# An MLP fused by row blocks, weight gradients as filler beside spectral stages, and transposes by DMA

## The chip, the cores and the metric

The kernel runs on one core of one Trainium2 chip. The metric is the device time of one execution in microseconds, the median of the runs shown.

## What is computed

A block with two halves, forward and backward (all gradients but that of B_x). With x of 2048 rows by 512 and mod = silu(c) @ w_mod, six vectors of 512 (sa, ca, ga, sb, cb, gb):

```python
h = _layernorm(x) * (1 + ca) + sa
x = x + ga * irfft2(rfft2(h) * (w_r + 1j * w_i))       # spectral half
h = _layernorm(x) * (1 + cb) + sb
r = relu(h @ w1 + b1)                                   # MLP half, 512 -> 1792 -> 512
x = x + gb * ((r * r) @ w2 + b2)
_out, _vjp = jax.vjp(_f, A_x, A_w_r, A_w_i, B_w1, B_b1, B_w2, B_b2, c, w_mod)
```

The inputs and outputs are bf16; grad_out goes into the vjp.

## The kernel before

TensorE is called PE here, VectorE DVE, ScalarE ACT, GpSimd POOL, SyncE SP. Rows are held as 128 partitions by 16 row tiles t; the inner width 1792 is 14 chunks fc of 128, the outer width 512 four chunks dc. Tiles are placed and ordered by a framework: the program gives each instruction an engine and a priority (its place in the text, unless changed), and the order on each engine's queue is fixed when the program is built. Every DMA is issued from SP's queue.

The 2D FFTs are matmuls with sine tables. F1 (`spec_f1`) multiplies each row tile by TA; F2 and F3 (`spec_f23`) go over eight pairs of frequencies, with PSUM tiles psB and psC, and end in an elementwise complex product (`cmul`); G1 (`spec_g1`) writes CS; G2 and G3 (`spec_g23`) turn CS into row tiles, psT and psY. The tables LF, LG, Cf and Cd are made at the start (`build_lf`, `build_lg`, `build_cf`, `build_cd`), written to DRAM and loaded again for the backward half.

The stages run one after the other:

1. Layernorm of x, F1, the six vectors, the tables; F2, F3 and G1 forward.
2. G2, G3, the residual and the second layernorm, row by row (`y_cons`, L632). Each four rows are transposed on PE into h2T.
3. h = w1 * h2T for all 14 fc (L683), relu into rT (L686), square into hactT (L687), rT to DRAM (L690).
4. out = hactT * w2 (L725) row by row, with column sums by matmuls with ones (L740, L743). Transposes of w2 (L720) and of gB = grad_out * gb (L746) on PE.
5. For each fc: psg = w2T * gBT (L784), ghT = 2 * rT * psg (L787), rT transposed back on PE (L797), copied (L798), squared (L800), and the gradient of w2 (L803). The transpose of w1 (L812).
6. gh * w1^T row by row (L843) with the layernorm's backward and three column sums.
7. `emit_gmod_chunk` for the vectors sb, cb and ga: their part of the gradient of w_mod and of c. (gb is done after stage 4, sa and ca at the end.)
8. In two halves: ghT transposed on PE (L891), copied (L893, L896), and the gradient of w1 (L902), written out by L911.
9. Backward: tables reloaded, F1 to G1 with two complex products per pair (`ew_bwd`), then G2, G3 and the first layernorm's backward row by row (`gh1_cons`, L960), and the last two `emit_gmod_chunk`.

Of the kernel before, what the change touches and what calls it, by code (L numbers as in the profile page):

```python
# [43 lines left out]
def build_basic(tc, constp, g):  # L44
# [37 lines left out]
def build_ta(tc, K, cpool, g, pspool):  # L82
# [15 lines left out]
    TA = cpool.tile([P, P], BF16, name="TA")  # L98
# [3 lines left out]
    TAT = cpool.tile([P, P], BF16, name="TAT")  # L102
# [4 lines left out]
def build_cd(tc, K, g):  # L107
    nc = tc.nc
# [10 lines left out]
    v = g.tile([P, 4, D], I32, name="cd_v")  # L119
    for c in range(4):  # L120
        nc.vector.scalar_tensor_tensor(out=v[:, c, :], in0=fr, scalar=d2[:, c:c + 1], in1=off, op0=ALU.mult, op1=ALU.add)
    nc.vector.tensor_single_scalar(v, v, 1023, op=ALU.bitwise_and)
    sn = g.tile([P, 4, D], FP32, name="cd_sn")
    nc.scalar.activation(sn, v, AF.Sin, scale=TWO_PI / 1024, bias=K["npi"])
# [4 lines left out]
def build_cf(tc, K, cpool, g):  # L129
    nc = tc.nc  # L130
    dr = g.tile([P, D], I32, name="cf_dr")
    nc.gpsimd.iota(dr, pattern=[[2, D]], base=1, channel_multiplier=0)
    f4 = g.tile([P, 4], FP32, name="cf_f4")
    for i, b in enumerate((0, 128, 1, 129)):
        nc.vector.tensor_scalar(f4[:, i:i + 1], K["pidf"], float(b), None, op0=ALU.add)
    efc = g.tile([P, 4], FP32, name="cf_ef")
    nc.vector.memset(efc, EF_S)
    nc.vector.tensor_scalar(efc[:, 0:1], K["pidf"], 0.0, EF_S * (math.sqrt(0.5) - 1.0), op0=ALU.is_equal, op1=ALU.mult)
    nc.vector.tensor_scalar(efc[:, 0:1], efc[:, 0:1], EF_S, None, op0=ALU.add)
    nc.vector.tensor_scalar(efc[:, 3:4], K["pidf"], 127.0, EF_S * (math.sqrt(0.5) - 1.0), op0=ALU.is_equal, op1=ALU.mult)  # L140
    nc.vector.tensor_scalar(efc[:, 3:4], efc[:, 3:4], EF_S, None, op0=ALU.add)
    v = g.tile([P, 4, D], I32, name="cf_v")
    for i in range(4):
        nc.vector.tensor_scalar(v[:, i, :], dr, f4[:, i:i + 1], 768.0 if i < 2 else 512.0, op0=ALU.mult, op1=ALU.add)
    nc.vector.tensor_single_scalar(v, v, 1023, op=ALU.bitwise_and)
    sn = g.tile([P, 4, D], FP32, name="cf_sn")
    nc.scalar.activation(sn, v, AF.Sin, scale=TWO_PI / 1024, bias=K["npi"])
    Cf = cpool.tile([P, 4, D], BF16, name="Cf")
    for i in range(4):
        nc.vector.tensor_scalar(Cf[:, i, :], sn[:, i, :], efc[:, i:i + 1], None, op0=ALU.mult)  # L150
    K["Cf"] = Cf


def build_lf(tc, K, cpool, g):
    nc = tc.nc
    sm = g.tile([P, 16, 8], FP32, name="lf_sm")
# [38 lines left out]
    c, s = tr
    LF = cpool.tile([P, 6, 16, P], BF16, name="LF")
    L5 = LF.rearrange("p y g (a b) -> p y g a b", b=8)
    for y, (w, m) in enumerate(((c, 0), (s, 1), (s, 2), (c, 2), (c, 1), (s, 3))):
        nc.vector.tensor_tensor(L5[:, y], w, mk[:, m, :, None, :].broadcast_to([P, 16, 16, 8]), op=ALU.mult)
    for y, w, z in ((2, c, z0), (3, s, z0n), (5, c, z0n)):  # L200
        nc.vector.tensor_scalar(L5[:, y, 0, :, 4], w[:, 0, :, 4], z, None, op0=ALU.mult)
    K["LF"] = LF


def build_lg(tc, K, cpool, g):
    nc = tc.nc
    lam = K["lowf"]
    rl = g.tile([P, 1], FP32, name="lg_rl")
    nc.gpsimd.tensor_scalar(rl, lam, -1.0, 7.0, op0=ALU.mult, op1=ALU.add)
    e4 = g.tile([P, 1], FP32, name="lg_e4")  # L210
    nc.gpsimd.tensor_scalar(e4, lam, 4.0, None, op0=ALU.is_equal)
    e0 = g.tile([P, 1], FP32, name="lg_e0")
    nc.gpsimd.tensor_scalar(e0, lam, 0.0, None, op0=ALU.is_equal)
    ge4 = g.tile([P, 1], FP32, name="lg_ge4")
# [148 lines left out]
def spec_g23(tc, K, CS, consumer):  # L363
    nc = tc.nc
    with tc.tile_pool(name="tsb", bufs=3) as tpool, \
# [8 lines left out]
        for t in range(NT):  # L374
# [6 lines left out]
            if prev is not None:  # L381
                g3(*prev)
# [655 lines left out]
```

## Time and profile before

| | us |
|---|---|
| median of 3 runs | 773.96 (772.61 to 774.38) |
| the profiled execution, its own time | 772.14 |
| its span in the trace | 770.4 |
| PE busy | 576.6 (75%) |
| DVE busy | 445.3 (58%) |
| ACT busy | 251.4 (33%) |
| DMA queue, share of 16 engines | 36.8%, 92.2 MB |

Busy time is the time in which an engine has an instruction in work. Matmuls are pipelined, so a row's mean time of one is longer than the distance from one to the next. The granted clock (PEclk) is the share of 2.4 GHz that PE was given.

### The profile page before, as it was taken

The numbers are of one execution on the slowest core, as the hardware profiler recorded it, in microseconds if no ns is written. First come the engines' busy times: TensorE is split into PE (matmuls) and PEld (weight loads), VectorE is DVE, ScalarE is ACT, GpSimd is POOL, SyncE is SP. The second block draws the span as 40 slices with busy tenths as digits, with TensorE's granted clock in tenths as the row PEclk, the third lists the DMA queues.
The fourth block names the chain that finished last, engine by engine and source line by source line (L and its number), as shares of the span: only waits on it lengthen the run. The fifth ranks groups of instructions, "written<-read, shape, count | busy, mean of one in ns | idle before, by whom it ended". The sixth has DMA issues, their size and how long they took to land. (4 is left out here: it accounts for less than half of the span.)

```text
span 770.4 us, 9001 instructions
## 1 busy us (share of the span) xinstructions
PE 576.6 (75%) x3190; PEld 278.1 (36%) x3190; DVE 445.3 (58%) x1126; ACT 251.4 (33%) x404; POOL 48.6 (6%) x138
## 2 busy tenths in 40 slices
PE   1364997457999995999999879955989369397530
PEld 0221683123444332445444323313555146262100
DVE  7977456655744445544554469983131039649981
ACT  2454546335664111223323201113231045144210
POOL 6531002310000000000000000000000000000000
PEclk9995999858999998999999979975999779799855
DMA  7208964577334231412221252321008780321110
GB/s 300 82 27 321 227 158 139 177 210 254 137 136 137 83 101 56 165 69 76 95 71 42 43 163 83 102 75 43 25 25 328 234 250 1 129 91 42 41 54 27
DMA packets 70528, 92.78 MB, mean 120 GB/s; under 512 B 9938, under 2 KB 62804, under 8 KB 69460
## 3 DMA queue, kind: packets, MB, share of 16 engines
q1 hardware_dynamic: 70484, 92.22, 36.8%
q8 instruction: 25, 0.41, 0.2%
q14 instruction: 19, 0.16, 0.1%
HBM read 51.80 MB, written 40.39 MB: 120 GB/s over the span
## 5 line engine op out<-in xcount | busy, mean ns | idle before, releaser
L787 DVE SCALAR_TENSOR_TENSOR ghT<-rT_pf,twof,psg 128x512 bf16<-128x512 bf16 x56 | 40.7, 745 | 55.8 <-PE psg L784 55.6
L784 PE MATMUL psg<-gBT,w2T 128*128 128x512 bf16 x224 | 60.2, 387 | 1.8 <-ACT gwm L439 1.8
L683 PE MATMUL psH<-h2T,w 128*128 128x512 bf16 x224 | 55.1, 402 | 5.2 <-ACT rT L686 4.4
L843 PE MATMUL psh<-w1T,ghT 128*128 128x512 bf16 x224 | 56.3, 392 | 0.4 <-DVE ghT L787 0.4
L902 PE MATMUL psw<-ghn,h2b 128*128 128x448 bf16 x256 | 52.0, 355 | 3.6 <-DVE gw L909 3.6
L725 PE MATMUL psO<-w,hactT 128*128 128x512 bf16 x224 | 53.5, 379 | 0.8 <-ACT rT L686 0.8
L803 PE MATMUL psw<-gB,hnat 128*128 128x512 bf16 x224 | 50.8, 380 | 0.5 <-DVE hnat L800 0.5
L686 ACT ACTIVATE rT<-psH,b1col 128x512 bf16<-128x512 f32 x56 | 38.4, 687 | 22.1 <-PE psH L683 17.4
L687 DVE TENSOR_TENSOR hactT<-rT 128x512 bf16<-128x512 bf16 x56 | 23.7, 424 | 25.3 <-ACT rT L686 25.2
L683 PEld LDWEIGHTS <-w 128*128 128x128 bf16 x224 | 22.7, 101 | 37.0 <-issue 16.3
L843 PEld LDWEIGHTS <-ghT 128*128 128x128 bf16 x224 | 20.0, 100 | 39.8 <-issue 21.6
L798 ACT COPY rnat<-pstr 128x512 bf16<-128x512 bf16 x56 | 29.9, 587 | 11.7 <-PE pstr L797 9.7
L902 PEld LDWEIGHTS <-h2b 128*128 128x128 bf16 x256 | 24.7, 99 | 24.7 <-issue 4.4
L805 ACT CAST gw<-psw 128x512 bf16<-128x512 f32 x14 | 8.2, 585 | 73.8 <-PE psw L803 68.5
L803 PEld LDWEIGHTS <-hnat 128*128 128x128 bf16 x224 | 20.8, 98 | 29.4 <-DVE hnat L800 6.2
L846 ACT CAST gh<-psh 128x512 bf16<-128x512 f32 x16 | 9.4, 585 | 63.2 <-PE psh L843 63.2
L784 PEld LDWEIGHTS <-w2T 128*128 128x128 bf16 x224 | 21.1, 99 | 23.2 <-issue 6.9
L909 DVE CAST gw<-psw 128x448 bf16<-128x448 f32 x8 | 5.0, 624 | 42.3 <-PE psw L902 25.3
L725 PEld LDWEIGHTS <-hactT 128*128 128x128 bf16 x224 | 20.2, 98 | 24.6 <-issue 4.2
L308 POOL MEMSET AE<- 128x2 bf16 x6 | 0.3, 107 | 453.7 <-PE psw L902 441.5
L730 DVE TENSOR_TENSOR bo<-psO,b2b 128x512 bf16<-128x512 f32 x16 | 11.1, 691 | 27.6 <-PE psO L725 27.6
L891 PE MATMUL pstg<-ident,ghT 128*128 128x128 bf16 x224 | 21.0, 242 | 7.7 <-DVE ghn L893 4.0
(326 smaller groups left out, 1084.4 us busy)
## 6 DMA issues: line engine op xcount, KB each, us to landing
rT_dram<-rT SPq DMA_DIRECT2D x14, 512.0 KB, 2.6
rT_pf<-rT_dram SPq DMA_DIRECT2D x14, 512.0 KB, 3.2
w<-in_B_w_dram SPq DMA_DIRECT2D x2, 1792.0 KB, 8.9
wm<-in_w_mod_dram SPq DMA_DIRECT2D x4, 768.0 KB, 10.0
LF_dram<-LF SPq DMA_DIRECT2D x1, 3072.0 KB, 10.3
LG_dram<-LG SPq DMA_DIRECT2D x1, 3072.0 KB
wmc_pf<-in_w_mod_dram SPq DMA_DIRECT2D x6, 512.0 KB, 10.8
out_dram<-gwm SPq DMA_DIRECT2D x24, 128.0 KB, 1.7
```

The source lines that it names most:

```text
L683: nc.tensor.matmul(psH, lhsT=w1[:, dc, fc * P:(fc + 1) * P], rhs=h2T[:, dc, sc * 4 * P:(sc + 1) * 4 * P], start=(dc == 0), stop=(dc == 3))
L686: nc.scalar.activation(rT[:, sc * 4 * P:(sc + 1) * 4 * P], psH, AF.Relu, bias=b1col[:, fc:fc + 1])
L687: nc.vector.tensor_tensor(hactT[fc][:, sc * 4 * P:(sc + 1) * 4 * P], rT[:, sc * 4 * P:(sc + 1) * 4 * P], rT[:, sc * 4 * P:(sc + 1) * 4 * P ...
L725: nc.tensor.matmul(psO, lhsT=hactT[fc][:, t * P:(t + 1) * P], rhs=w2[:, fc, :], start=(fc == 0), stop=(fc == NFC - 1))
L730: nc.vector.tensor_tensor(bo, psO, b2b, op=ALU.add)
L784: nc.tensor.matmul(psg, lhsT=w2T[:, dc, fc * P:(fc + 1) * P], rhs=gBT[:, dc, sc * 4 * P:(sc + 1) * 4 * P], start=(dc == 0), stop=(dc == 3))
L787: nc.vector.scalar_tensor_tensor(out=ghT[fc][:, sc * 4 * P:(sc + 1) * 4 * P], in0=rT[:, sc * 4 * P:(sc + 1) * 4 * P], scalar=K["twof"], in ...
L798: nc.scalar.copy(out=rnat[:, 4 * tg:4 * tg + 4, :], in_=pst.rearrange("p (j f) -> p j f", j=4))
L803: nc.tensor.matmul(psw2, lhsT=hnat[:, t, :], rhs=gB[:, t, :], start=(t == 0), stop=(t == NT - 1))
L843: nc.tensor.matmul(psh, lhsT=ghT[fc][:, t * P:(t + 1) * P], rhs=w1T[:, fc, :], start=(fc == 0), stop=(fc == NFC - 1))
L891: nc.tensor.transpose(pst[:, jj * P:(jj + 1) * P], ghT[fc][:, t * P:(t + 1) * P], K["ident"])
L902: nc.tensor.matmul(psw, lhsT=h2[:, t, dc * P:(dc + 1) * P], rhs=ghn[:, t, cc * 448:(cc + 1) * 448], start=(t == 0), stop=(t == NT - 1))
```

## The change

- g * w2^T is taken apart from the relu's derivative: `gaT = (2 gb w2)^T g` needs no forward result and is computed beside the forward spectral stages, with a priority of LATE behind all else. Its operands gT and w2T come by DMA with `transpose=True`.
- The MLP runs in four blocks of four row tiles: `stage_g` (G2, G3, second layernorm, h2T by PE as before), `stage_h` (h, relu, square, `gaT *= r`), `stage_o` (out, gh * w1^T, layernorm's backward, F1 of the backward half for the last blocks). w1T comes by DMA transpose and is scaled and centred in place, so that the layernorm's mean term needs no pass of its own. h and gh go to DRAM.
- The gradients of w1 and w2 are computed beside the backward spectral stages, again LATE, from h and gh loaded back by DMA transposes (ghn, hn). The column sums of sb and cb come out of w1's gradient instead of matmuls with ones.
- `GMod.emit` makes the gradient of w_mod by scaling one broadcast row on ACT in place of four outer products on PE.
- The tables are smaller (LF 4 rows and LFx, LG by windows and LGx) and made in pieces; the complex products take one tile per pair; column sums are issued some rows later (`Delayed`).

```diff
+class Priority:
...
+    def __enter__(self):
+        self.tc.cur_priority = self.tc.cur_priority + self.shift
...
+class Delayed:
...
+    def add(self, fn):
+        self.q.append(fn)
+        if len(self.q) > self.lag:
+            self.q.pop(0)()
...
+    def emit(self, jc, row_ap, pool, ppool, wmc):
+        psb = ppool.tile([P, D], FP32, name="mm")
+        nc.tensor.matmul(psb, lhsT=K["ones_row"], rhs=row_ap, start=True, stop=True)
...
+        nc.scalar.copy(out=gmbc, in_=psb)
...
+        for dc in range(4):
+            nc.scalar.activation(gwm[:, dc, :], psb, AF.Copy, scale=self.scf[:, dc:dc + 1])
+            nc.vector.scalar_tensor_tensor(out=junk, in0=wmc[:, dc, :], scalar=K["onef"], in1=gmbc, op0=ALU.mult, op1=ALU.mult,
+                                           accum_out=self.gsc[:, jc, dc:dc + 1])
+        nc.sync.dma_start(self.out9_view[:, :, jc * D:(jc + 1) * D], gwm)
...
+    for b in range(NB):
+        gT.append(w2gp.tile([P, 4, SB], BF16, name="gT", bufs=2))
+        for j in range(TB):
+            nc.sync.dma_start(gT[b][:, :, j * P:(j + 1) * P], g_view[:, TB * b + j, :], transpose=True)
+        if b == 0:
+            nc.sync.dma_start(w2T, B_w2, transpose=True)
...
+    with Priority(tc, LATE):
+        for dc in range(4):
+            nc.vector.tensor_scalar(w2T[:, dc, :], w2T[:, dc, :], gb2x[:, dc:dc + 1], None, op0=ALU.mult)
+        for b in range(NB):
+            for fc in range(NFC):
+                ps = mmps.tile([P, SB], FP32, name="mm")
+                for dc in range(4):
+                    nc.tensor.matmul(ps, lhsT=w2T[:, dc, fc * P:(fc + 1) * P], rhs=gT[b][:, dc, :], start=(dc == 0), stop=(dc == 3))
+                with tc.high_priority():
+                    if fc % 2 == 0:
+                        nc.vector.tensor_copy(out=gaT[fc][:, b * SB:(b + 1) * SB], in_=ps)
+                    else:
+                        nc.scalar.copy(out=gaT[fc][:, b * SB:(b + 1) * SB], in_=ps)
...
+    nc.sync.dma_start(w1T, B_w1, transpose=True)
...
+        def stage_h(b):
...
+            for fc in range(NFC):
+                ps = mmps.tile([P, SB], FP32, name="mm")
+                for dc in range(4):
+                    nc.tensor.matmul(ps, lhsT=w1[:, dc, fc * P:(fc + 1) * P], rhs=h2T[b][:, dc, :], start=(dc == 0), stop=(dc == 3))
...
+                nc.scalar.activation(r, ps, AF.Relu, bias=b1col[:, fc:fc + 1])
...
+                nc.vector.tensor_tensor(h, r, r, op=ALU.mult)
+                nc.sync.dma_start(h_dram[fc, :, sl], h)
+                nc.vector.scalar_tensor_tensor(out=gaT[fc][:, sl], in0=r, scalar=K["onef"], in1=gaT[fc][:, sl],
+                                               op0=ALU.mult, op1=ALU.mult, accum_out=gb1acc[:, fc, b:b + 1])
+                nc.sync.dma_start(gh_dram[fc * P:(fc + 1) * P, sl], gaT[fc][:, sl])
...
+        stage_g(0)
+        stage_g(1)
+        stage_h(0)
+        stage_o(0)
+        stage_g(2)
+        stage_h(1)
+        stage_o(1)
+        stage_g(3)
...
+    def grad_w2():
+        for fc in range(NFC):
+            hn = gwp.tile([P, NT, P], BF16, name="hn", bufs=2)
+            nc.sync.dma_start(hn, h_dram[fc, :, :], transpose=True)
+            ps = mmps.tile([P, SB], FP32, name="mm")
+            for t in range(NT):
+                nc.tensor.matmul(ps, lhsT=hn[:, t, :], rhs=g_sb[:, t, :], start=(t == 0), stop=(t == NT - 1))
+            gw = gwp.tile([P, D], BF16, name="gw", bufs=3)
+            with tc.high_priority():
+                nc.vector.tensor_tensor(gw, ps, modb[:, GB_B, :], op=ALU.mult)
+            nc.sync.dma_start(out6_view[:, fc, :], gw)
+    def grad_w1():
...
+        W4 = 256
+        for fb in range(F // W4):
+            ghn = gwp.tile([P, NT, W4], BF16, name="ghn", bufs=2)
+            nc.sync.dma_start(ghn, gh_dram[fb * W4:(fb + 1) * W4, :], transpose=True)
...
+            for dc in range(4):
...
+                    nc.tensor.matmul(ps[:, 0:W4], lhsT=n2_sb[:, t, dc * P:(dc + 1) * P], rhs=ghn[:, t, :],
+                                     start=(t == 0), stop=(t == NT - 1))
...
+    with Priority(tc, LATE):
+        for j, row in ((5, ggb_row), (2, gga_row)):
+            wmc = gm.prefetch(j, gwp)
+            gm.emit(j, row, gwp, mmps, wmc)
+        grad_w1()
...
+        spec_f23(tc, K, UT, CdB, None, lambda gi: fr.tile([P, 2, 2, FP], BF16, name="G"), ew_b)
...
+    spec_g1(tc, K, Z, CS)
...
+    with Priority(tc, LATE):
+        grad_mod_mid()
+        grad_w2()
```

Not shown of the diff: the tables, `stage_g` and `stage_o` (per row: o0 = o * gb + x1, gp = g * o, then cb, a scalar_tensor_tensor with the sum of cb * n2, u = rb * n2 + g, gx1 = u + cb, qy = gx1 * y), and the last rows' arithmetic, in which two scalar_tensor_tensors become tensor_tensors. In `stage_g` psT, psY and the transposes' pst2 have one PSUM buffer each, in F2 psB has one in place of two. w2, w1 and w1T are in the space of w2T, gT and the forward Z.

## Rows read from the trace of the kernel before

**Rows 1.** Busy time, granted clock and DMA by stage (start:end in us).
```profile
0.00:56.00 56.00, 20.32 (x120) 9.97 (x121) 47.08 (x117) 23.37 (x29) 30.19 (x85) 0.99 0.36 132
56.00:117.00 61.00, 48.15 (x321) 32.67 (x320) 35.91 (x81) 27.47 (x35) 4.82 (x19) 0.84 0.83 231
117.00:166.00 49.00, 26.03 (x144) 11.54 (x143) 32.84 (x89) 22.25 (x39) 13.44 (x32) 0.81 0.54 167
166.00:226.00 60.00, 54.77 (x232) 22.98 (x230) 32.81 (x88) 37.78 (x56) 0.00 (x0) 0.90 0.53 193
226.00:298.00 72.00, 68.69 (x371) 28.68 (x370) 34.15 (x82) 18.22 (x34) 0.00 (x0) 1.00 0.31 101
298.00:308.00 10.00, 3.26 (x14) 1.02 (x14) 5.70 (x15) 1.52 (x3) 0.00 (x0) 0.65 0.16 53
308.00:431.00 123.00, 121.59 (x732) 59.24 (x732) 61.23 (x142) 37.71 (x70) 0.00 (x0) 0.99 0.24 82
431.00:505.00 74.00, 65.24 (x260) 21.29 (x258) 57.89 (x165) 9.95 (x17) 0.00 (x0) 0.93 0.37 105
505.00:530.00 25.00, 9.61 (x26) 2.27 (x26) 17.61 (x49) 5.46 (x10) 0.00 (x0) 0.58 0.22 74
530.00:605.00 75.00, 67.12 (x470) 40.37 (x470) 16.02 (x35) 20.25 (x36) 0.00 (x0) 0.93 0.31 122
605.00:622.00 17.00, 0.90 (x7) 0.39 (x6) 0.62 (x1) 0.00 (x0) 0.17 (x3) 0.59 0.98 268
622.00:657.00 35.00, 34.01 (x254) 23.58 (x252) 27.28 (x54) 20.80 (x31) 0.00 (x0) 0.95 0.28 84
657.00:686.00 29.00, 16.55 (x132) 13.77 (x131) 13.91 (x27) 4.95 (x10) 0.00 (x0) 0.76 0.37 146
686.00:740.00 54.00, 34.86 (x112) 9.34 (x112) 50.45 (x154) 18.12 (x33) 0.00 (x0) 0.85 0.10 34
740.00:770.40 30.40, 5.49 (x10) 0.99 (x9) 11.74 (x37) 3.51 (x6) 0.00 (x0) 0.50 0.13 43
sum 770.40, PE 576.59 PEld 278.09 DVE 445.27 ACT 251.36 POOL 48.63; mean PE 38.44 PEld 18.54 DVE 29.68 ACT 16.76 POOL 3.24
```
**Rows 2.** Pace of PE: timeline of F3, then chain of waits in the w1 gradient.
```profile
74.38 3.62 PE L317 MATMUL psC<-AE,LF 128*128 128x257 bf16 x16 [11.52 <-ACT AE L333]
...
80.19 1.95 PE L317 MATMUL psC<-AE,LF 128*128 128x257 bf16 x16
...
541.63 0.49 PE pstg L891 x8
542.12 0.57 PE psw L902 x3
...
546.12 20.63 PE psw L902 x109
```
**Rows 3.** Pace of DVE: timeline in the last rows, then a copy from the groups.
```profile
689.89 0.74 DVE L968 SCALAR_TENSOR_TENSOR gn<-psY,onef,modb 128x512 bf16<-128x512 f32 x1
690.56 0.08 DVE L968 DVE_READ_ACCUMULATOR gn<-psY,onef,modb 128x1 f32 x1
690.65 0.42 DVE L965 TENSOR_TENSOR q<-gh,n1b 128x512 bf16<-128x512 bf16 x1
690.99 0.74 DVE L971 SCALAR_TENSOR_TENSOR qn<-gn,onef,n1b 128x512 bf16<-128x512 bf16 x1
...
L358 DVE CAST CS<-psG 128x512 bf16<-128x512 f32 x8 | 5.5, 690 | 6.5 <-PE psG L351 6.5
```
**Rows 4.** DMA issues: times, KB each, median us from issue to landing.
```profile
out_dram<-gwm SPq DMA_DIRECT2D x24, 128.0 KB, 1.7
...
Wb<-in_A_w_i_dram SPq DMA_DIRECT2D x1, 1028.0 KB, 11.9
...
b1colb<-in_B_b_dram SPq DMA_DIRECT2D x1, 3.5 KB, 3.3
```
**Rows 5.** The chain that ended last: a store of w1's gradient.
```profile
584.23 8.45 DMA out_dram<-gw
```

More of the change, by code (lines that the diff above doesn't have):

```diff
@@ L24 @@
 NT = 16
+NB = 4
+TB = NT // NB
+SB = TB * 128
 P = 128
@@ L142, in build_cf @@
[L142 to L147, printed above, removed]
+    efc = g.tile([P, 2], FP32, name="cf_ef")
+    for i, edge in enumerate((0.0, 127.0)):
+        nc.vector.tensor_scalar(efc[:, i:i + 1], K["pidf"], edge, math.sqrt(0.5) - 1.0, op0=ALU.is_equal, op1=ALU.mult)
@@ L195, in build_lf @@
[L195 to L202, printed above, removed]
+    LF = cpool.tile([P, 4, 16, P], BF16, name="LF")
@@ L284, in spec_f1 @@
-def spec_f1(tc, K, row, UT):
-    nc = tc.nc
-    with tc.tile_pool(name="psA", bufs=3, space=PSUM) as psA_pool:
-        for t in range(NT):
-            hrow = row(t)
-            ps = psA_pool.tile([P, 4, P], FP32, name="psA")
-            for c in range(4):
-                nc.tensor.matmul(ps[:, c, :], lhsT=hrow[:, c * P:(c + 1) * P], rhs=K["TA"], start=True, stop=True)
-            dst = UT[:, :, :, t, :]
-            src = ps.rearrange("p c (a b) -> p c a b", b=8)
-            if t % 2 == 1:
-                nc.scalar.copy(out=dst, in_=src)
-            else:
-                nc.vector.tensor_copy(out=dst, in_=src)
+    mk = g.tile([P, 2, 6, 8], BF16, name="lg_mk")
@@ L300, in spec_f23, with spec_f1_row @@
+def spec_f1_row(tc, K, hrow, t, UT, pool, name):
+    nc = tc.nc
+    ps = pool.tile([P, 4, P], FP32, name=name)
+    for c in range(4):
+        nc.tensor.matmul(ps[:, c, :], lhsT=hrow[:, c * P:(c + 1) * P], rhs=K["TA"], start=True, stop=True)
+    dst = UT[:, :, :, t, :]
+    src = ps.rearrange("p c (a b) -> p c a b", b=8)
+    if t % 4 == 0:
+        nc.vector.tensor_copy(out=dst, in_=src)
+    else:
+        nc.scalar.copy(out=dst, in_=src)
 def spec_f23(tc, K, UT, Cd, dc, dest, elementwise):
@@ new lines, with grad_mod_mid @@
+    gsba = gwp.tile([P, 4, F // 256], FP32, name="gsba")
+    gcba = gwp.tile([P, 4, F // 256], FP32, name="gcba")
+    def grad_mod_mid():
+        for i, j in enumerate((3, 4)):
+            wmc = gm.prefetch(j, gwp)
+            psr = psX.tile([P, D], FP32, name="mm")
+            for dc in range(4):
+                nc.tensor.matmul(psr[0:1, dc * P:(dc + 1) * P], lhsT=colsb[:, i, dc:dc + 1], rhs=K["ident"], start=True, stop=True)
+            row = gwp.tile([1, D], BF16, name="gmrow")
+            nc.scalar.copy(out=row, in_=psr[0:1, :])
+            gm.emit(j, row, gwp, psX, wmc)
```

1292 lines of the change are left out of this document (590 added, 702 removed).

## The prediction

> **What bounds the kernel now.** I read the profile in this order: time by stage, the pace of TensorE (PE), the pace of VectorE (DVE), the DMA rows, the chain that ended last. In the table by stage [rows 1] the reader is to see that no engine bounds the whole: PE is busy 576.6 us of 770.4 and DVE 445.3, but they take turns. PE is full in the MLP stages (121.6 of 123 us in 308 to 431) and mostly idle in the setup, where the setup and the tables are made (20.3 of 56), in the stage of G2, G3 and the second layernorm (26.0 of 49), in the modulation gradients (9.6 of 25), while weights are reloaded (0.9 of 17) and in the last two stages, of which 686 to 740 is DVE's (50.5 of 54). So what a change saves is read stage by stage: work taken off PE counts in the MLP stages, and work put into the spectral stages is free only as far as PE really is idle there.
>
> PE's pace [rows 2]: 109 matmuls of 448 columns take 20.63 us, 0.189 us each, 0.42 ns a column; so 0.216 us for 512 columns, 0.108 for 256. Eight transposes take 0.49 us, 0.061 each. These are at the full clock; the same 16 matmuls of F3 take 1.95 us, and 3.62 when PE has just been idle for 11.5 us: in such a stretch the granted clock falls to half (0.50 in 740 to 770.4, 0.58 in 505 to 530 [rows 1]), which is 1.2 of 2.4 GHz.
>
> What the five PE-bound stages lose: at that pace 166 to 226 holds 48.9 us of matmuls (224 and 8 transposes), 226 to 298 holds 62.1 (256 and 112 transposes), 308 to 431 113.9 (448 and 280), 431 to 505 58.8 (272), 530 to 605 62.1 (256 of 448 columns and 224). That is 345.8 us of columns in 404 us: a stage bound by PE runs at 0.856 of PE's pace. I use this below as the measured efficiency of such stages.
>
> DVE's pace [rows 3], start to start: a scalar_tensor_tensor of 128x512 0.67 us, with its accumulator read 0.76; a bf16 tensor_tensor 0.34. A copy out of PSUM has a mean of 0.69 us [rows 3], and by the same 0.08 of overlap a pace of 0.61.
>
> **The change part by part.** The new order has three parts: A, up to the end of the forward G1, with g*w2^T as filler; B, the MLP forward and backward in four blocks of four row tiles; C, backward spectral, with both weight gradients as filler.
>
> *Removed everywhere.* 624 transposes on PE (224 of rT, 224 of ghT, 56 each of w2 and w1, 64 of gB): 38 us, with the copies out of PSUM behind them. Also 32 column sums and 24 outer products of 512 columns, 12 us. Added on PE: 16 bias rows and 56 one-column matmuls, 7 us, and 96 one-column ones in the setup.
>
> *A.* Before: 117 us. g*w2^T is 224 matmuls, 48.4 us. It needs the scaled w2T, so the modulation, which is made last in the setup stage. After 56 us PE is idle for 61 - 48.2 = 12.8 us [rows 1]; the other 35.6 lengthen the part: 153. Against that I take 10 us for the setup: the layernorm makes 4 round trips to GpSimd instead of 16, and the LG and Cf tables come after LF. Bounds of this: 0 (DVE is busy 47.1 of 56 us [rows 1] and most of that stays) and 18 (DVE's 8.9 us of idle time, and as much again for tables that move behind). Another 4 us because filled gaps keep the clock up (the 3.62 against 1.95 us [rows 2]; it was 0.84 of full in 56 to 117 [rows 1]). A = 139. The 28 copies of g*w2^T on each of DVE (0.61) and ScalarE lie beside it: DVE has about 100 us of 139.
>
> *B.* Before, 117 to 505: 388 us. PE afterwards: 816 matmuls of 512 columns (G2, G3 80; h, out and gh*w1^T 224 each; bias 16; column sums 48) are 176.3 us; 64 transposes, 64 of F1 and 56 small ones 11.2; together 187.5. DVE: G-stage 32.8 [rows 1], h-stage 56 x (0.34 + 0.76) = 61.6, out-stage 16 x (5 x 0.34 + 0.76 + 0.67 + 0.1) = 51.7, w1T's scaling 28 x 0.33 = 9.2, F1 2.4: 158. So PE sets it by a little. 187.5 / 0.856 = 219. Before the first h can run, four rows of G2/G3 with layernorm must pass, at the 49 / 16 = 3.1 us per row of that stage [rows 1]; PE can do little beside them: 10 us more. w2, w1 and w1T (5.5 MB) can only load once g*w2^T and Z have given up their space; eight rows, 24 us, cover them at 230 GB/s; at 177 GB/s they take 31, 7 us more. B = 229.
>
> *C.* Before, 505 to 770.4: 265 us. PE: 407 matmuls of 512 columns (F2, G2, G3, column sums, w2's gradient, broadcasts) 87.9, 704 of 256 (F3, G1, and w1's gradient in 448) 76.0: 164, by 0.856 192. DVE: 41.2 for spectral work as in 622 to 686; 50.5 - 16 x 0.85 = 37 for the last rows (two scalar_tensor_tensors become a tensor_tensor each); w1's gradient 84 x 0.40 + 56 x 0.09 = 38.6 (256 columns, not in the trace: between half of 0.67 and all of it, nearer the half, as the time goes with the columns); w2's 8.5; modulation 18.2: 144, hidden. At the start some 5 MB of tables, W and g come before the first product, 16 us at 268 GB/s [rows 1], 6 of it covered: 10. The end: one buffer holds both last slices of w_mod, so the second one loads after the first is used: two passes and a load, 15 us against the 30.4 now. C = 217.
>
> *Transposes by DMA.* No row shows one. 20 MB: g and w2 (3.8) in A, w1 (1.8) in B, h and gh (14.7) in C. Nothing is lost if they are fast. Bounds: above, plain loads, 268 GB/s [rows 1]; below, the rows with the shortest runs: b1 in 2-byte elements, 3.5 KB in 3.3 us [rows 4], 1 GB/s, with which nothing would end. I take the strided W loads, 1028 KB each, two at once in 11.9 us [rows 4]: 177 GB/s, as a transpose also reads short runs but hundreds of bytes long. 14.7 MB are then 83 us, and C's other 31 MB (tables, g, x's and W's rows, outputs) at 268 GB/s 117: 200 us within C's 217. Just hidden. All DMAs are on SP's queue, so loads and stores stand behind each transpose; a store that stands behind loads is what the chain now shows for 8.45 us before a gradient buffer is free [rows 5]. I price this at nothing in the sum (gw has 3 to 4 buffers in place of 2), up to 3 x 8 us in the range.
>
> **The sum.** 139 + 229 + 217 = 585 us of span. The profiled run took 772.14 us, 1.7 over its span, and the median of the runs is 773.96, 1.0024 of it: 585 + 1.7, times 1.0024, is 588.
>
> **Rivals.**
> 1. *Transposes bound C.* At half the rate, 88 GB/s: 166 + 117 + 15 = 298 us, +81: 669. For it: at 177 GB/s the margin is 17 us. Against: loads and stores in that part need not all wait for each other.
> 2. *Slower than before: the transposes are so slow that they alone decide.* The place is C, where PE's queue holds the gradient matmuls in a written order and waits for hn and ghn. The point: C may take 217 + 186 = 403 us, so 403 - 15 - 117 = 271 for 14.7 MB, 54 GB/s. Price if each 128x128 block costs what a small plain DMA needs to land, 1.7 us [rows 4]: 448 x 1.7 = 762, C = 762 + 117 + 15 = 894, 1,265 in all. For it: the 1 GB/s of 2-byte elements shows that the form of a transfer can cost that much. Against: W's strided rows run at 177 GB/s. A rule of the Trainium skill speaks for this rival: "VectorE: DVE Perf Modes", The three transpose paths, gives 1309 ns for a 128x128 block by DMA against 390 ns on TensorE. The trace disagrees with it on TensorE's side, with 0.061 us a transpose in a row of them [rows 2], and no run here shows the DMA side yet; were 1309 ns the pace of many, C's 448 blocks would be 586 us and the kernel some 1,090, an estimate from that page.
> 3. *The filling does not happen*, as the written order puts fillers where PE was not idle. A = 103 + 48.4 / 0.856 = 160, B as separate stages less what is removed (14 us) 241, C = 57 (spectral stages) + 40 (last rows) + 113 (97 us of gradient matmuls by 0.856) + 10 + 15 = 235: 636 of span, 639. For it: an order fixed at build time stalls at the first late tile. Against: the order built now already interleaves, three of w1's gradient matmuls behind each eight transposes [rows 2].
> 4. *Better*: all parts reach the 0.926 of 308 to 431: A 132, B 202, C 192: 526 and so 529.
>
> **How the numbers follow.** Forecast 0.50, rival 1 0.20, rival 2 0.12, rival 3 0.13, rival 4 0.05. The prediction is 588. The range leaves out rival 2, the end of rival 1 (under 68 GB/s) and half of rival 4: 530 to 720. The forecast's own, from the bounds (A 135 to 153, B without its 10 or with 7 more, C up to 24 more), is 574 to 633. A change under 0.2% can't be told from none by these runs. Faster 0.86 (all but rival 2 and 0.02 of rival 1 that end near the time now), the same 0.02, slower 0.12.
>
> **What would show it.** Right: PE busy above 80% in the middle of the run; no matmul of a gradient waiting for hn or ghn; transposes that land at over 150 GB/s; g*w2^T interleaved with F2 and F3; a granted clock near 1.0 from 60 us on. Wrong: idle time of PE ended by DMAs into ghn, hn, w1T or gT (rivals 1 and 2), or PE idle in C with these tiles there (rival 3), or B bound by DVE or by single PSUM buffers of G2 and G3 rather than by PE.

## The result, and the profile after

The changed kernel takes 625.58 us, the median of 4 runs (623.48 to 628.68), against 774.01 for the kernel before on the same chip: a ratio of 0.8088, 95% interval 0.805 to 0.8127. The profiled execution took 626.75, with a span of 624.9. The forecast was 588, with a range of 530 to 720. Each ratio is to the kernel before on the same chip. On another chip the changed kernel measured 0.7958 (0.7927 to 0.7989). The runs of one group below (1 to 4, 5 to 8, 9 and 10, 11 and 12) shared a chip; a kernel is set against the changed one by these ratios or, where both ran in one group, directly. Kernels 1 to 4 had no changed kernel beside them, so what they gain is given from 0.7958 and from 0.8088.

Busy time by stage of the changed kernel, columns as in [rows 1]: part A ends at 116 us, part B's last row product at 351, then a hole to 376, then part C.

```profile
37.00:101.00 64.00, 58.23 (x314) 30.71 (x319) 53.07 (x147) 39.65 (x67) 5.46 (x38) 1.00 0.60 162
101.00:116.00 15.00, 14.94 (x133) 13.02 (x133) 8.85 (x16) 4.69 (x8) 0.00 (x0) 1.00 0.56 158
116.00:160.00 44.00, 38.84 (x221) 17.68 (x225) 25.45 (x61) 22.31 (x40) 8.71 (x20) 1.00 0.48 153
160.00:351.00 191.00, 178.04 (x836) 73.32 (x852) 136.16 (x377) 71.02 (x110) 6.10 (x14) 0.98 0.63 174
351.00:376.00 25.00, 1.75 (x10) 0.85 (x10) 4.02 (x9) 1.27 (x2) 0.00 (x0) 0.60 0.73 117
376.00:423.00 47.00, 35.74 (x192) 20.11 (x195) 35.49 (x73) 17.35 (x30) 0.00 (x0) 0.86 0.91 250
423.00:446.00 23.00, 18.20 (x138) 14.63 (x139) 13.90 (x34) 8.75 (x16) 0.00 (x0) 0.90 1.13 212
446.00:491.00 45.00, 31.31 (x149) 12.71 (x150) 37.85 (x123) 29.13 (x65) 0.00 (x0) 0.87 0.64 181
491.00:545.00 54.00, 49.19 (x414) 41.06 (x414) 38.55 (x148) 13.42 (x27) 0.00 (x0) 0.92 0.66 139
545.00:625.00 80.00, 57.06 (x218) 22.23 (x221) 21.57 (x48) 12.42 (x21) 0.00 (x0) 0.85 0.69 148
sum 625.00, PE 499.51 PEld 256.55 DVE 402.23 ACT 238.99 POOL 30.11; mean PE 45.41 PEld 23.32 DVE 36.57 ACT 21.73 POOL 2.74
```

PE is busy 499.5 us for 576.6 before, and idle 125 us for 194: a little over half of what is saved is work taken off PE, the rest idle time. PE's pace is that of [rows 2] (14 matmuls of 512 columns in 3.13 us in the chain, 0.22 each). The forecast's three parts were 139, 229 and 217 us; measured are 116, 260 (with the hole) and 249.

The same view for the product g*w2^T alone (PE busy and its count, granted clock, DMA): it fills F2 and F3, and what is left of it fills the first rows of the MLP part.

```profile
37.00:101.00 64.00, 29.77 (x124) 1.00 0.60 162
101.00:116.00 15.00, 0.81 (x3) 1.00 0.56 158
116.00:160.00 44.00, 22.62 (x86) 1.00 0.48 153
```

The chain that ended last answers to [rows 5]. Where it held a store of 8.45 us before, it now holds one of 28.43 us at the end of B, two issues of transposes on SP's own queue (SPq) in C, and loads of hn in the tail:

```profile
329.23 3.13 PE og L781 x14
...
342.46 0.43 DVE u L809
342.91 28.43 DMA gx_dram<-u
...
434.87 6.79 SPq L895
441.72 4.96 SPq L895
...
546.74 4.63 DMA hn<-h_dram
...
585.33 13.90 DMA hn<-h_dram
...
621.70 0.69 DVE gw L885
```

DMA issues, answering to [rows 4] (KB each, us to landing), and below them, for ghn's transposes, how long the issue itself takes on SP (min/median/max in ns, first and last start in us):

```profile
LGb<-LG_dram SPq DMA_DIRECT2D x1, 1792.0 KB, 33.5
...
gT<-in_grad_out_dram SPq DMA_TRANSPOSE x16, 3.4
hn<-h_dram SPq DMA_TRANSPOSE x14, 5.1
...
ghn<-gh_dram SPq DMA_TRANSPOSE x7, 7.3
...
out_dram<-gb1b SPq DMA_DIRECT2D x1, 3.5 KB
```

```profile
L895 SPq DMA_TRANSPOSE ghn<-gh_dram x7: 3855/4177/6794, 434.9 to 527.9; - x7
```

Two holes stand out, and the busy table shows the same at the start of both: DMA engines fully busy that move almost nothing.

```profile
342.00:346.00 4.00, 3.94 (x22) 1.55 (x20) 3.31 (x8) 0.69 (x1) 0.00 (x0) 1.00 1.90 32
...
588.00:592.00 4.00, 0.76 (x4) 0.14 (x2) 0.69 (x1) 0.00 (x0) 0.00 (x0) 0.95 1.05 8
```

The first begins some 8 us after two stores of gb1, the bias gradient (out_5 at 333.49 us, and a copy in memory that C reads back, at 334.86), the second some 10 us after the store of the gradient of c (578.61). Each of these writes its numbers one by one, 2 bytes each, 1,792 or 512 of them; such a store is called scattered here. Between the first two and the hole the table LGb is reloaded as well (issued at 336.77). SP's own queue also waits for both stores of gb1 to land before it issues a store of gx and a load of y (us in total, times, longest):

```profile
SPq L810 <- DMA out_dram<-gb1b: 9.2, 1, 9.2
...
SPq L813 <- DMA gb_dram<-gb1b: 6.7, 1, 6.7
```

The reload, the scattered stores, the transposes, too few buffers and a bound by VectorE are the suspects that the runs set apart.

### The profile page after: what moved, and what is told of

The parts are those of the page before. It is cut to its first block, busy times and chain, and to the rows that moved or that the text cites. A ratio compares the mean times of both kernels' runs of the same rounds, so it can differ in the third digit from the quotient of the medians.

```text
span 624.9 us, 8582 instructions
## 1 busy us (share of the span) xinstructions
PE 499.5 (80%) x2803; PEld 256.5 (41%) x2844; DVE 402.2 (64%) x1133; ACT 239.0 (38%) x415; POOL 30.1 (5%) x112
## 4 chain that ended last, share of the span: by engine, by line
DMA 20%; PE 20%; DVE 12%; SPq 3%; issue 2%; ACT 0%; POOL 0%; DVEq 0%; ACTq 0%; POOLq 0%
DMA hn<-h_dram 7%; PE mm L900 5%; PE mm L882 5%; DMA gx_dram<-u 5%; DMA out_dram<-gW 3%; PE og L781 3%; PE mm L763 2%; DMA ghn<-gh_dram 2%; PE og L799 2%; SPq L895 2%; DVE p L408 1%; DVE gaT L770 1%; DVE p L409 1%; DMA Wb<-in_A_w_r_dram 1%; DVE jk L992 1%
## 5 line engine op out<-in xcount | busy, mean ns | idle before, releaser
L882 PE MATMUL mm<-g_sb,hn 128*128 128x512 bf16 x219 | 58.1, 421 | 19.4 <-DMA hn<-h_dram 19.0
L640 PE MATMUL mm<-gT,w2T 128*128 128x512 bf16 x217 | 54.4, 378 | 8.3 <-DVE gaT L643 5.7
L900 PE MATMUL mm<-ghn,n_sb 128*128 128x256 bf16 x448 | 54.6, 282 | 7.5 <-DVE gw L912 5.1
L781 PE MATMUL og<-w,h 128*128 128x512 bf16 x217 | 55.9, 386 | 3.6 <-DVE h L768 3.3
L763 PE MATMUL mm<-h2T,w 128*128 128x512 bf16 x220 | 57.0, 386 | 0.2
L900 PEld LDWEIGHTS <-n_sb 128*128 128x128 bf16 x448 | 44.7, 101 | 20.4 <-issue 11.7
L799 PE MATMUL og<-w1T,gaT 128*128 128x512 bf16 x218 | 51.5, 380 | 0.3
L765 ACT ACTIVATE r<-mm,b1col 128x512 bf16<-128x512 f32 x56 | 38.3, 687 | 30.5 <-DVE gaT L770 22.7
L770 DVE SCALAR_TENSOR_TENSOR gaT<-r,onef,gaT 128x512 bf16<-128x512 bf16 x56 | 41.8, 746 | 0.0
L781 PEld LDWEIGHTS <-h 128*128 128x128 bf16 x224 | 20.4, 98 | 30.4 <-DVE h L768 6.5
L390 PE MATMUL psT<-Cf,utcs 128*128 128x512 bf16 x123 | 32.6, 379 | 0.2
L907 ACT ACTIVATE gtmp<-gb1bc,mcol 128x256 f32<-128x256 bf16 x28 | 14.1, 509 | 39.3 <-DVE gw L912 34.8
L807 DVE SCALAR_TENSOR_TENSOR u<-n2rows,rb,gb 128x512 bf16<-128x512 bf16 x16 | 12.0, 752 | 22.6 <-DMA gx_dram<-u 22.0
```

What stands on the lines that cost most here:

```text
L390: nc.tensor.matmul(ps, lhsT=CS[:, t, c].rearrange("p r a b -> p (r a b)"), rhs=K["Cf"][:, c, :], start=(c == 0), stop=(c == 3))
L640: nc.tensor.matmul(ps, lhsT=w2T[:, dc, fc * P:(fc + 1) * P], rhs=gT[b][:, dc, :], start=(dc == 0), stop=(dc == 3))
L763: nc.tensor.matmul(ps, lhsT=w1[:, dc, fc * P:(fc + 1) * P], rhs=h2T[b][:, dc, :], start=(dc == 0), stop=(dc == 3))
L765: nc.scalar.activation(r, ps, AF.Relu, bias=b1col[:, fc:fc + 1])
L770: nc.vector.scalar_tensor_tensor(out=gaT[fc][:, sl], in0=r, scalar=K["onef"], in1=gaT[fc][:, sl], op0=ALU.mult, op1=ALU.mult, accum_out=gb ...
L781: nc.tensor.matmul(ps, lhsT=hT[b, fc][:, j * P:(j + 1) * P], rhs=w2[:, fc, :], start=(fc == 0), stop=False)
```

## The experiments

**1. The bias gradient in rows.**

```diff
-            nc.sync.dma_start(out5_view, gb1b)
-            nc.sync.dma_start(gb1_dram.rearrange("(fc p) -> p fc", p=P), gb1b)
...
+        nc.tensor.transpose(pgb[0:NFC, 0, :], gb1b, K["ident"])
...
+        nc.vector.tensor_copy(gb1t, pgb[0:NFC, 0, :])
+        nc.sync.dma_start(out_5.rearrange("(fc p) -> fc p", p=P), gb1t)
+        nc.sync.dma_start(gb1_dram.rearrange("(fc p) -> fc p", p=P), gb1t)
```

> The gradient of the bias (gb1, 1,792 numbers) is transposed on TensorE and stored as 14 rows of 256 bytes, in place of two stores of 1,792 single numbers of 2 bytes; nothing else changes. Theory 1 (the two scattered stores hold the DMA queue from 334 to 365 us, and with it the last stores and reloads of the MLP part): the PE idle of 22 us before 372 us goes, and the time falls by 18 to 25 us. Theory 2 (the reload of the 1,792 KB table LGb, which lands in 33.5 us in the same stretch, holds the queue): the time stays within 5 us, and the store of gx1 that waited 28 us still waits over 15 us. Theory 3 (the stretch is filled by all transfers together): 5 to 12 us.

603.41 us, ratio 0.7837 (0.7802 to 0.7872). What F1 of the backward part waited for, and the reload, in its trace:

```profile
  DVE u L809: 2.4, 1
```

```profile
LGb<-LG_dram SPq DMA_DIRECT2D x1, 1792.0 KB, 8.0
```

In the changed kernel this wait is 23.4 us (15.3 in the run of it on the other chip, and 10.9, 11.4, 12.9 and 13.2 in kernels 2, 3, 4 and 7, which keep the two stores). The reload of LGb is still there and lands in 8.0 us for 33.5, so it was held itself: for the wait, theory 1. The gain in time is 9 us from 0.7958 and 19 from 0.8088, as the stall itself varies; the first would fit theory 3 too, and kernel 12 decides between them.

**2. Plain loads for the transposes.** The two loads in the gradients lose `transpose=True` and read rows of the same blocks.

> The loads of h and of gh for the two weight gradients keep their bytes, but are plain loads of rows, without the transpose; the gradients are then products of the untransposed blocks, the matmul counts stay. Theory 1 (the transposing loads set the pace of the tail: the w2 gradient waits 19 us for hn, the w1 gradient for ghn, and the DMA queue's sequencer needs 2 to 7 us to issue each): the time falls by 20 to 40 us and the w2 gradient runs at its matmul pace, about 50 us for 79 us. Theory 2 (the w2 gradient waits because only two buffers of hn exist, so that a load begins when a product ends, whatever its kind): a fall of 5 to 12 us, with waits for hn of 1 to 3 us each left. Theory 3 (TensorE and VectorE set this part): within 3 us.

599.42 us, ratio 0.7766 (0.7722 to 0.781). Its loads of the same bytes land in 5.7 and 4.6 us, for 7.3 and 5.1 as transposes, and SP needs 0.38 us to issue one instead of 4.18:

```profile
ghn<-gh_dram SPq DMA_DIRECT2D x7, 1024.0 KB, 5.7
hn<-h_dram SPq DMA_DIRECT2D x14, 512.0 KB, 4.6
```

```profile
L895 SPq DMA_DIRECT2D ghn<-gh_dram x7: 377/377/1247, 419.9 to 507.4; - x7
```

The w2 gradient still takes 67 us from its first to its last matmul, and waits 10.3 us for hn in 7 waits: near theory 2. The gain is 15 us from 0.7958 and 25 from 0.8088. The wait ahead of C is shorter too, 10.9 us for 15.3 and 23.4, though the edit does not touch it. Less that, 10 to 12 us are left: an estimate of what all the transposes of C cost.

**3. Six places for hn.**

```diff
-            hn = gwp.tile([P, NT, P], BF16, name="hn", bufs=2)
+            if fc % 6 < 2:
+                hn = gwp.tile([P, NT, P], BF16, name="hn", bufs=2)
+            else:
+                if fc % 2 == 0:
+                    hn2 = gwp.tile([P, NT, 256], BF16, name="ghn", bufs=2)
+                hn = hn2[:, :, (fc % 2) * P:(fc % 2 + 1) * P]
```

> The w2 gradient's blocks of h get six places instead of two: the four others lie in the two buffers of ghn, which are free by then; the transposing loads stay as they are. Theory 1 (each load waits for its buffer, and its 5 us latency shows): the 19 us of waits for hn fall below 6 us, the time by 12 to 25 us. Theory 2 (the transposes are bound by their rate: 512 KB in 5 us, one after the other, against 3.5 us of matmuls): the waits fall to no less than 12 us, the time by under 8 us.

603.34 us, ratio 0.7829 (0.7794 to 0.7864), a gain of 10 us from 0.7958 and 20 from 0.8088. No matmul waits for hn any more, so the rate of the transposes is enough: theory 1 for the waits; its gain of 12 to 25 us is met only from 0.8088. Now another thing ends the tail. SP's queue in this run, then the chain, then the busy time in a stretch of it:

```profile
567.88 0.37 SPq L1029 DMA_DIRECT2D out_dram<-gcb  x1
568.30 0.77 SPq L891 DMA_DIRECT2D out_dram<-gw  x1
569.16 6.40 SPq L884 DMA_TRANSPOSE hn<-h_dram  x1
```

```profile
568.30 16.46 DMA out_dram<-gw
```

```profile
574.00:578.00 4.00, 3.33 (x16) 1.39 (x15) 0.00 (x0) 0.00 (x0) 0.00 (x0) 1.00 1.49 10
```

Right behind the scattered store of the gradient of c (gcb) a store of 128 KB takes 16.46 us, for 1.7 in [rows 4], while 10 GB/s move; gw's three buffers run out and PE waits 9.5 us. So not all of the changed kernel's waits for hn were a want of places; the longest of them lies in the second hole (us in total, times, longest):

```profile
PE mm L882 <- DMA hn<-h_dram: 19.0, 8, 10.5
```

**4. A quarter of g*w2^T.**

```diff
-                for dc in range(4):
-                    nc.tensor.matmul(ps, lhsT=w2T[:, dc, fc * P:(fc + 1) * P], rhs=gT[b][:, dc, :], start=(dc == 0), stop=(dc == 3))
+                nc.tensor.matmul(ps, lhsT=w2T[:, 0, fc * P:(fc + 1) * P], rhs=gT[b][:, 0, :], start=True, stop=True)
```

> Only one of the four matmuls of each block of g*w2^T is left, the other three (168 matmuls, 36 us at 216 ns) are left out; its evictions and loads stay. Theory 1 (the product fills gaps, as it was forecast): the forward spectral stages end at the same 116 us and the time falls by no more than 8 us. Theory 2 (40% of it spills into the MLP part, which has no gaps to fill, and a part of it delays the spectral stages): the time falls by 15 to 28 us. Theory 3 (no filling): a fall of 36 us.

618.01 us, ratio 0.7989 (0.7943 to 0.8036), no less than the changed kernel's 0.7958 to 0.8088: 36 us of matmuls left out, and no gain to be told. The total is as theory 1 has it, but the stages are not: in the profiled execution, the longest of its four, G1 ends at 132 us, not at 116, at a granted clock of 0.73 where the changed kernel has 1.00.

```profile
37.00:117.00 80.00, 54.80 (x243) 25.85 (x245) 60.49 (x159) 46.48 (x78) 5.98 (x39) 0.73 0.45 130
...
133.00:168.00 35.00, 23.26 (x109) 8.00 (x111) 18.19 (x55) 9.46 (x17) 3.26 (x9) 0.53 0.78 209
```

Over the whole span the clock is 0.88 to 0.91 in its four executions, for 0.92 to 0.94 in the changed kernel's. So the matmuls left out changed the clock as well, and this run doesn't tell whether they were free.

Kernels 5 to 8 ran on one chip, with the changed kernel among them.

**5. Three edits together**: those of 1 and 3, and the gradient of c turned on PE and stored as 4 rows of 256 bytes.

```diff
-            nc.sync.dma_start(out8_view, gcb)
...
+        nc.tensor.matmul(pgc[0:4, 0:P], lhsT=gcb, rhs=K["ident"], start=True, stop=True)
+        nc.vector.tensor_copy(gca_t[0:4, 0:P], pgc[0:4, 0:P])
+        nc.sync.dma_start(out_8.rearrange("b (dc p) -> (b dc) p", p=P), gca_t[0:4, 0:P])
```

> Three edits at once on the changed kernel: the bias gradient stored in rows of 256 bytes, six places for the blocks of h, and the gradient of c (512 numbers, until now one store of single numbers) also stored in rows of 256 bytes. Theory 1 (each removes its own stall: 20 us at the end of the MLP part, 13 us of waits for hn, 10 to 16 us around 570 to 590 us, where the stores of the w2 gradient stand behind the scattered store of the gradient of c): 574 to 584 us. Theory 2 (the third stall is the end of the transposes and not the scattered store): 588 to 595 us.

**6. The changed kernel again.**

> The changed kernel as it is, on this chip: a ratio of 0.805 to 0.813 to the kernel before. The idle of TensorE ended by the first rows of the backward spectral part (23 us in the first profile, 11 to 13 us in runs whose edits don't touch that stretch) shows how much this stall varies from run to run.

**7. No filling.** The scaling of w2T and the loops of the product move from their late priority to behind `spec_g1(tc, K, Z, CS)`, at the priority of that place, and wait for it:

```diff
-    with Priority(tc, LATE):
-        for dc in range(4):
-            nc.vector.tensor_scalar(w2T[:, dc, :], w2T[:, dc, :], gb2x[:, dc:dc + 1], None, op0=ALU.mult)
...
+    nc.vector.scalar_tensor_tensor(out=gb2x, in0=CS[:, 15, 3, 1, 7, 0:4], scalar=0.0, in1=gb2x, op0=ALU.mult, op1=ALU.add)
+    for dc in range(4):
+        nc.vector.tensor_scalar(w2T[:, dc, :], w2T[:, dc, :], gb2x[:, dc:dc + 1], None, op0=ALU.mult)
...
```

> The product g*w2^T loses its late priority and is held behind the last evictions of the forward spectral stages: its weights' scaling takes a value (times zero) from their result. It then runs as one block ahead of the MLP part. Theory 1 (as a filler it took gaps of the spectral stages and of the MLP rows, where the kernel before had TensorE idle): the time rises by 25 to 45 us. Theory 2 (it only moves the work: VectorE's evictions bound the forward stages and the MLP part): under 10 us. The forward spectral stages alone end at 100 to 116 us if the filler cost them something, later if the granted clock falls without it.

**8. The w1 gradient behind the spectral stages**, on top of 5:

```diff
             gm.emit(j, row, gwp, mmps, wmc)
-        grad_w1()
...
     with Priority(tc, LATE):
+        grad_w1()
         grad_mod_mid()
         grad_w2()
```

> The three edits of the kernel in three parts, and the w1 gradient, with its loads (n2, w1, gb1, gh), is put behind the backward F2, F3 and G1 stages in the order of the program. Theory 1 (its loads of 8 MB ahead of the blocks of W and X hold the F2 and F3 stages, where the transfers are busy at 92 to 113%, while its products fill only 8 us there): the backward spectral stages end 8 to 15 us earlier and the total falls by 2 to 8 us against the three edits alone. Theory 2 (the products that ran there, and the loads made early, are worth more): the total rises by 3 to 10 us.

Measured: kernel 5 584.81 us (0.7586, 0.7552 to 0.7621), kernel 6 613.84 (0.7958), kernel 7 646.33 (0.8376, 0.8342 to 0.8409), kernel 8 585.89 (0.759).

Kernel 5 is 29 us below the changed kernel (31 by the two spans): 13 at the end of B (a wait of 2.4 for 15.3 us) and 19 in the w2 gradient, which takes 57 us for 76. In kernel 3, with the places alone, that gradient takes 66 us, so places and the store of gcb are worth some 10 us each there. The time lies 1 us above theory 1's range and below theory 2's; the stall behind gcb is gone, so it is theory 1. Kernel 7 costs 32.5 us: as a filler, the product saved two thirds of its 48.4 us. Its rows show the second thing that the filler does:

```profile
37.00:94.00 57.00, 33.37 (x194) 19.53 (x193) 41.62 (x129) 30.28 (x51) 5.96 (x38) 0.74 0.54 168
...
110.00:165.00 55.00, 54.65 (x285) 24.05 (x285) 21.97 (x33) 16.34 (x28) 0.00 (x0) 0.97 0.15 37
```

Without the filler, F2 and F3 run at a granted clock of 0.74 (0.97 in kernel 6 and 1.00 in the first profile with it) and PE is busy 33.37 of 57 us. That idle time takes in most of the filler: some 30 us of its matmuls run there, and G1 ends only 8 us later (118 us in kernel 6, 109 in kernel 7). Kernel 8 changes nothing, as its edit does not move what it was to move: with the late priority SP issues the w1 gradient's loads where kernel 5 does (n2 at 380 to 381 us, w1 at 397 to 398, the first gh at 414 in both). Neither of its theories is tested by it.

The backward part is not filled, and why is the next question. The w1 gradient alone in kernel 5 (PE busy, count):

```profile
357.00:421.00 64.00, 0.00 (x0) 0.92 0.97 244
421.00:440.00 19.00, 3.03 (x18) 0.91 0.99 265
440.00:472.00 32.00, 4.11 (x30) 0.79 0.49 134
472.00:520.00 48.00, 45.74 (x400) 0.96 0.87 172
```

7 of 53 us of it run before the spectral work ends at about 472 us. Its first transposes are issued at 414, and afterwards, in the last rows, DVE is full (all engines, columns as in [rows 1]):

```profile
440.00:472.00 32.00, 18.13 (x91) 7.17 (x90) 31.11 (x103) 19.09 (x44) 0.00 (x0) 0.79 0.49 134
```

**9. The w2 gradient as the filler**, on top of 5 (`load_hn` is the load of experiment 3, made once for each fc):

```diff
             gm.emit(j, row, gwp, mmps, wmc)
-        grad_w1()
...
             nc.sync.dma_start(Xt[gi][:, :, :, 0:DF], xs_dram[:, gi, :, :, 0:DF])
+            if 1 <= gi <= 6:
+                load_hn(gi - 1)
+        with Priority(tc, LATE):
+            grad_w2()
...
     with Priority(tc, LATE):
+        grad_w1()
         grad_mod_mid()
-        grad_w2()
```

> On top of the three edits the two gradients change places: the w2 gradient, whose blocks need one VectorE operation of 0.69 us for 3.5 us of matmuls, becomes the filler of the backward spectral stages, with its first six transposing loads of h issued between the loads of W and X; the w1 gradient (four VectorE or ScalarE operations for a block of 1.9 us) follows, with the two slices of the gradient of w_mod that need its sums. Theory 1 (the w1 gradient could not fill because its first transpose was issued only 57 us into the part and because VectorE is full in these stages): the w2 gradient fills 20 us or more of TensorE's 31 us of idle time, and the total falls by 8 to 20 us against the three edits alone, after 10 to 15 us are given back at the end for the two slices. Theory 2 (the fill only displaces: transposes hold W and X, or VectorE is the bound of the part): the total rises by up to 15 us.

**10. The w1 gradient's loads early**, on top of 5:

```diff
-    nc.sync.dma_start(g_sb, g_view)
+    nc.sync.dma_start(n2_sb, n2_dram)
...
+            if gi == 1:
+                load_ghn(0)
+                nc.sync.dma_start(gb1bc, gb1_dram[None, :].to_broadcast((P, F)))
+            elif gi == 2:
+                nc.sync.dma_start(w1n, w1_view)
+            elif gi == 4:
+                load_ghn(1)
```

> On top of the three edits the w1 gradient stays the filler, but what it needs is loaded early: n2 in the place of the 2 MB of g (which only the w2 gradient needs, and which goes behind), the first block of gh and gb1 after the second block of W and X, w1 after the third, the second block of gh after the fifth. Theory 1 (late loads alone kept it from filling): w1 products start before 385 us for 424 us, over 10 us of them run before 421 us, and the total falls by 6 to 12 us against the three edits. Theory 2 (VectorE, busy 44 of 51 us between 370 and 421 us, can't take the extra 1.4 us for each block of 1.9 us): the spectral stages end later by about as much as is filled, and the total stays within 3 us.

Kernel 9: 579.06 us, 0.7499 (0.7469 to 0.7528). Kernel 10: 587.53 us, 0.7605 (0.7572 to 0.7638). The w2 gradient alone in kernel 9:

```profile
357.00:421.00 64.00, 13.85 (x52) 0.92 0.98 218
421.00:440.00 19.00, 1.42 (x5) 0.97 0.97 317
440.00:472.00 32.00, 14.07 (x56) 0.97 0.77 223
```

29 us are filled, as theory 1 of 9 has it, and both gradients end at 546.6 us for 577. But 30 us follow, and the spectral stages themselves end later: G1 at 428 us for 421, the last row at 487 for 475. So only 6.7 us come out by the ratios, less than the 8 to 20 of theory 1. In kernel 10 the w1 gradient starts at 376 and puts 7.8 us into F2 and F3, G1 ends at 429, and the total is within 3 us of kernel 5: theory 2 of 10. Up to G1 the two fillers thus put the stages off by about the same; the difference lies in the last rows. From 440 to 472 us 14.1 us of w2's gradient run in kernel 9 and 5.3 us of w1's in kernel 10. There DVE is what the stage lacks: a block of w1's takes 1.9 us of PE and 1.4 of DVE, one of w2's 3.5 and 0.69. With w1's gradient as the filler, early data alone didn't shorten the kernel; w2's gradient without its early loads was not run.

**11. Kernel 9 with its end reordered**, in one group with 12:

```diff
         gm.emit(1, gca_row, gwp, psX, wmc1)
+        wmcs = [gm.prefetch(j, gwp, True) for j in (3, 4)]
+        grad_mod_mid(wmcs)
...
         grad_w1()
-        grad_mod_mid()
```

With True, `prefetch` takes a tile of hn's name and size.

> The kernel with the w2 gradient as filler, and the last slices of the gradient of w_mod reordered: in it both weight gradients ended at 546.8 us, and 28 us followed in which four slices took turns on one buffer (3.7 us of load and 8 VectorE operations of 0.77 us each). The two slices that don't need the w1 gradient's sums now come before, the other two get their loads early, in the buffers of h that are free by then. Theory 1 (the turns on the buffer are the tail): the span ends 13 to 18 us earlier, 560 to 567 us in all. Theory 2 (the VectorE work of the slices is the tail, wherever it is put): 572 us or more.

**12. The same with one scattered store back.**

```diff
+            nc.sync.dma_start(out5_view, gb1b)
...
-        nc.sync.dma_start(out_5.rearrange("(fc p) -> fc p", p=P), gb1t)
```

> The same kernel as the run beside it, with one of the scattered stores put back: the output of the bias gradient again goes out as 1,792 single numbers of 2 bytes (the copy that the next part reads stays in rows). Theory 1 (each scattered store holds the queue by itself for some 10 us): 7 to 14 us more, with the idle of TensorE ahead of the backward spectral part back at 8 to 14 us. Theory 2 (the stall came from what waited for the copy in memory, or from both stores together): under 3 us more.

Kernel 11: 570.99 us, 0.7398 (0.7371 to 0.7424), the best here. The gain over 9 is 7.8 us by the ratios, between the theories: the last slices end 15 us after the w1 gradient instead of 30, but that ends 6 us later, with one wait of 6.97 us for ghn. Kernel 12: 576.54 us, 0.7471 (0.7452 to 0.7489), 5.5 us more beside it. Its chain has the hold back, at 13.88 us for the 16 to 28 of the kernels with two such stores:

```profile
345.07 13.88 DMA gx_dram<-u
```

F1 waits 10.4 us instead of 2.4. One scattered store is enough, as theory 1 has it; the total rises a little less than its 7 to 14 us.

## Why the prediction was right in sign and short by 6%

**Part A, 139 forecast, 116 measured.** Two terms are mis-sized. "The other 35.6 lengthen the part": 22.6 of the product's 54.4 us went to the first MLP rows, where PE was idle too, and most of the rest fitted gaps, so F2 to G1 take 79 us for 61. And the setup, priced at 10 us less with bounds of 0 and 18, is 19 us shorter: F2 starts at 36.8 us for 55.9. The 4 us for the clock were right in kind (0.74 in kernel 7 for 0.97 to 1.00); no run gives their size.

**Part B, 229 forecast, 235 to the last row product.** It took in those 22.6 us as well, so PE's columns went at a better pace than 0.856: 187.5 + 20 us of columns in 235, 0.88. A and B together were to be 368 us; 351 had passed at B's last row product. The terms for PE hold.

**The step that failed** is the price of nothing for stores behind others on the DMA queue ("I price this at nothing in the sum", with "up to 3 x 8 us in the range"). Their place wasn't the gradient buffers alone: the scattered stores at the end of B (11 to 23 us on PE) and of the gradient of c (16 us for a store, 9.5 on PE) held what stood behind them. The row of b1 in [rows 4], 3.5 KB in 3.3 us, was used as a bound for transposes; it is a load of the same form as these stores, and the kernel before had stored gb1 in that form too. Asking what the same form costs as a store, with the next part's data behind it, was the question missed. The trace of the kernel before had the answer: SP waits 13.9 us at the very end for the 1 KB of gcb, issued at 754.3 us (the same wait for the last store of the changed kernel, 128 KB of gw, is 1.1 us), and the store of gwm issued 0.6 us behind it lands in 14.5 us, for 1.7 of the two before it (the wait, then the issues from 754.8 to 757 us):

```profile
SPq L1033 <- DMA out_dram<-gcb: 13.9, 1, 13.9
```

```profile
out_dram<-gwm SPq DMA_DIRECT2D x1, 128.0 KB, 14.5
```

Yet the DMA engines show no traffic from 756.5 us to the end at 770.4: what is held there is the landing, the report that the store is done, and not the bytes. Behind the scattered store of gb1 in that kernel (424.6 us) a store of 128 KB landed in 12.4 us and loads of 128 KB, with 1.5 MB of others beside them, in 12.9 to 14.1, and PE stood still for 8.0 us. So 13.9 of the 30.4 us that the prediction reads as its last slices were one such store, and the other may have cost up to 8 us more.

**Part C, 217 forecast, 249 measured, 222 in kernel 5.** Two errors offset each other in kernel 5: the filling failed (7 of 53 us), as rival 3 has it, and the 15 us for the slices of w_mod at the end fell away, as they ran beside w2's gradient, which set the end. In the changed kernel 19 us of waits for hn come on top, about half for want of places and half behind the store of gcb. What rival 3 did not have is that the fill was lost to VectorE and to late loads; in kernel 11, with w2's gradient as the filler, C is 567.5 - 355 = 212. That kernel 5's three parts (116, 242, 222: 580) meet the sum of 585 is therefore partly chance.

**The transposes** (177 GB/s forecast). 1 MB of ghn in 7.3 us is 144 GB/s, 512 KB of hn in 5.1 us 103; below the 150 that I named, and yet worth only some 10 us by run 2, as the same bytes in plain loads land at 184 and 114. Rivals 1 and 2 fall. The Trainium skill, "VectorE: DVE Perf Modes", The three transpose paths, would have 1309 ns for a block of 128x128; 32 blocks of ghn in 7.3 us are 0.23 us each, so the trace disagrees with it as the pace of many. The Trainium skill, "Advanced Engine Details and Errata", X-Bar Transpose (TRN2), has transposes as fast as plain DMAs: landing times 1.1 and 1.3 times as long here are nearer to that, though far from the rate that it gives, and SP's issue time of 4.18 against 0.38 us isn't in it.

**What would show it.** PE over 80% in mid-run, the product among F2 and F3, and the clock near 1.0 from 60 us on (0.98 to 1.00 up to 351): seen. Gradient matmuls without waits for hn: not seen (19.0 us). The sign was never near: without filling (kernel 7) and with all stalls the time is still 0.8376 of before.

**Open.** Why the same two stores cost 11 us in one run and 23 in another; that they hold the queue is shown by taking them away and putting one back, what they do inside it is not. Scattered stores where nothing stands behind them weren't tried. Of the changes that saved time, only the forward filler was taken back (kernel 7); what the blocks and the transposes taken off PE bring is read from busy times alone.

## What to carry to other kernels

Before a sum ends with queues at nothing, look for stores whose elements lie apart in memory: turn them into rows on TensorE first, which costs one small matmul and a copy. Choose a filler by what the stage lacks: a product with few evictions beside rows that VectorE bounds. And when loads show as waits, try more places for them, also in tiles that are free by then, before blaming their rate.

## What the runs showed of the hardware

- One store of 3.5 KB in 2-byte pieces held a later store for 13.88 us, two of them for 15.9 to 28.4 us, and one of 1 KB a store behind it for 16.46 us, with DMA engines shown busy at 8 to 32 GB/s. At the end of the kernel before, a store of 128 KB right behind one of 1 KB landed in 14.5 us for 1.7, though the DMA engines showed no traffic after the first 1.6 us of it. A load of b1 in such pieces landed in 3.3 us [rows 4].
- A transposing DMA occupied the issuing queue for a median of 2.5 us (512 KB) or 4.2 us (1 MB), a plain load of 1 MB for 0.38 us.
- Work put into idle PE time also kept the clock up: the granted clock of F2 and F3 was 0.74 without the filler, between the two levels of 1.2 and 2.4 GHz, and 0.97 to 1.00 with it.
